# Windowed attention into a gated MLP: the third unit's transposes and outputs one step later, and both parts of the root's diagonal on VectorE

## The chip, the cores and the metric

The kernel runs on one core of a Trainium2 chip. The metric is device microseconds of one launch; the median of three runs is given. A profiled execution of its own supplies the trace that the text reads. Engines are named as in the profile: PE is TensorE's matmul stream, PEld its weight loads, DVE is VectorE, ACT ScalarE, POOL GpSimd, SP SyncE, which here issues the DMAs.

## The reference

```python
def reference(q, k, v, w_gate, w_val, w_out, rms_g):      # q, k, v: 8 x 8 heads x 576 x 64
    scores = q @ k.T / 8                                   # per batch and head
    # heads 0-3: keys 0..31 back; heads 4-7: keys 0, 4, 8, .. 124 back
    attn = softmax(where(mask, scores, -1e9))
    x = concat_heads(attn @ v)                             # 4608 tokens x 512
    xn = x / sqrt(mean(x * x, -1) + 1e-6) * rms_g
    g = xn @ w_gate                                        # 512 x 1536
    return (g * sigmoid(g) * (xn @ w_val)) @ w_out         # 1536 x 512
```

All is float32.

## The kernel before

The 4608 tokens are cut into 16 units of 288 (half a batch each). A unit has an attention part and an MLP part. The MLP of a unit takes 12 blocks j of 128 hidden columns, and each block takes three steps called ticks: a gate tick (12 matmuls into the PSUM tile g), a val tick (12 into v) and a projection tick (12 into the four accumulators acc, for the block before). The first unit (u = 0) uses float32 weights; from u = 1 on every product is made of three fp32r products of high and low parts (names ending in hi and lo).

The attention of unit u+1 runs inside the ticks of unit u's MLP. It consists of 14 bursts, one for each pair of heads and block of queries. A burst (c, i) passes through three stages on PE at three ticks: scores s (L509, or L512 from u = 3), transposes of the weights t (L487) and outputs o (L496, or L500 and L501). Lists of ticks set when: `q_at`, `t_at` and `o_at`. Units below NEX = 3 do their attention in plain float32, so "the third unit" (u = 2, NNAT = 2) is the last with float32 attention and the first whose attention runs beside fp32r MLP matmuls. Within a tick PE has the 12 MLP matmuls first, then the burst work.

What the other engines do for a tick is put off with `later(dt, rank, fn)`: at the start of a later tick `flush()` issues what is due, in order of rank. Ranks that matter here: a SwiGLU product (prod) has 0, the transposes' copy out of PSUM (untranspose, tile pt) 0.2, the addition of squares 0.4, the output copy (take, tile xraw) 0.5, silu 0.6, the maximum of the scores (scores_max, L379 and L384) 0.7. Each engine runs its own list strictly in order.

A transpose writes either into the free end of the g or v bank of that tick or, in a projection tick, into a PSUM tile of its own.

At the end of a unit's attention stands its root. `rms_sum` sums the squares on PE (rps, L560); `rms_root` adds epsilon on DVE (L567), takes the power -1/2 on POOL (rst, L568), and splits it on POOL into rst_hi (L573) and rst_lo (L574). `spread` makes of each part three 96 x 96 diagonals, the tiles rd_0 and rd_1, one on DVE (L582, one instruction) and one on ACT (L586, three instructions). Two matmuls with a matrix of ones (L602, bps) then broadcast the root over the partitions, and four DVE instructions (L616) scale x with it. The bps matmuls stand on PE behind the gate group of the eleventh block (g_10), two ticks after rps; the scores of a burst of the next attention (s_0_2) stand just ahead of g_10.

On POOL the root's two small instructions are followed by hlo (L723, low part of the hidden block) and by qs (L362, low part of a head's queries).

Of the kernel before, what the change touches and what calls it, by code (L numbers as in the profile page):

```python
# [9 lines left out]
F32 = mybir.dt.float32  # L10
# [3 lines left out]
AF = mybir.ActivationFunctionType  # L14
ALU = mybir.AluOpType
# [10 lines left out]
QB = 96  # L26
NC = DM // P
NJ = FF // P
NNAT = 2
NEX = 3  # L30
# [31 lines left out]
def geometry(u, c):  # L62


    half = u % 2
    if c < NC // 2:
        if half:
            return [(QB * i, QB * i, 0, P) for i in range(U // QB)], QB, U + W
        return [(QB * i, max(QB * i - W, 0), 0 if i else W, P if i else QB)
                for i in range(U // QB)], QB, U  # L70
    nq = U // DIL
    keys = nq + (W if half else 0)
    return [(nq * r, keys * r, 0 if half else W, keys) for r in range(DIL)], nq, keys * DIL
# [3 lines left out]
def attn_moe(ctx: ExitStack, tc: tile.TileContext, qk_in, v_in, w_gate, w_val, w_out, rms_g, outT):  # L77
# [4 lines left out]
    V, A, G, PE = nc.vector, nc.scalar, nc.gpsimd, nc.tensor  # L82
# [6 lines left out]
    ident = cst.tile([QB, QB], F32, name="ident")  # L89
# [29 lines left out]
    def later(dt, rank, fn):  # L119
        put_off.setdefault(now[0] + dt, []).append((rank, fn))  # L120
# [182 lines left out]
    def further(b, n):  # L303

        k = everything.index(b) + n
        return everything[k] if k < len(everything) else None
# [129 lines left out]
    def add(u, c, i, o):  # L436
        _, nq, _ = geometry(u, c)
        x = xraw[u, c]
        to = x[:, QB * i:QB * i + nq] if c < NC // 2 else x.rearrange("p (j r) -> p r j", r=DIL)[:, i, :]
        for a in range(2):  # L440
            rows = slice(a * D, (a + 1) * D)
            V.tensor_tensor(out=to[rows], in0=o[rows, a * nq:(a + 1) * nq], in1=to[rows], op=ALU.add)  # L442
# [18 lines left out]
    def untranspose(b, t_ps, wait):  # L461
        blocks, nq, _ = geometry(*b[:2])
        n = blocks[b[2]][3]
        t_in = t_ps[:n].rearrange("k (a q) -> k a q", a=2)[:, :, :nq]
        exact = b[0] < NEX
        st[b] = pt = sb.tile([P, 2, 2, QB], F32 if exact else F32R, tag="pt", name=f"pt_{b[0]}_{b[1]}_{b[2]}", bufs=2)
        A.copy(out=pt[:n, 0, :, :nq], in_=t_in)  # L467
        def low_part():
            V.tensor_tensor(out=pt[:n, 1, :, :nq], in0=t_in, in1=pt[:n, 0, :, :nq], op=ALU.subtract)

        if not exact:
            later(1, 0.4 if wait > 1 else -1.5, low_part) if wait else low_part()

    def products(q, t, o, t_ps, s_tag="s", o_tag="o", wait=0):


        if q:
            s_ps = ps.tile([P, 512], F32, tag=s_tag, name=f"s_{q[0]}_{q[1]}_{q[2]}")
        if o:
            o_ps = ps.tile([P, 512], F32, tag=o_tag, name=f"o_{o[0]}_{o[1]}_{o[2]}")  # L480
            pt = st.pop(o)
        if t:
            p, _ = st.pop(t)
        def transposed(a):
            blocks, nq, _ = geometry(*t[:2])
            n = blocks[t[2]][3]
            PE.transpose(t_ps[:n, a * QB:a * QB + nq], p[:nq, a, :n], ident[:nq, :nq])  # L487

        def output(a):
            blocks, nq, _ = geometry(*o[:2])  # L490
            n = blocks[o[2]][3]
            if a:
                return
            out = o_ps[:, :2 * nq].rearrange("d (a q) -> d a q", a=2)
            if o[0] < NEX:
                PE.matmul(out, vs.pop(o)[:n].rearrange("k a d -> k (a d)"), pt[:n, 0, :, :nq], start=True, stop=True)  # L496
                return
            vh, vl = (part[:n].rearrange("k a d -> k (a d)") for part in vparts[everything.index(o) % 2])
            both = o_ps[:, :4 * nq].rearrange("d (t a q) -> d t a q", t=2, a=2)
            PE.matmul(both, vh, pt[:n, :, :, :nq], start=True, stop=False)  # L500
            PE.matmul(out, vl, pt[:n, 0, :, :nq], start=False, stop=True)  # L501

        def scored(a):
            blocks, nq, _ = geometry(*q[:2])
            qc, kc, _, n = blocks[q[2]]
            sv = s_ps[:QB].rearrange("q (a t k) -> q a t k", a=2, t=2)
            if q[0] < NEX:
                qk = heads[q[0], 2 * q[1] + a]
                PE.matmul(sv[:nq, a, 0, :n], qk[:, qc:qc + nq], qk[:, U + kc:U + kc + n], start=True, stop=True)  # L509
                return  # L510
            qs, ks = heads[q[0], 2 * q[1] + a]
            PE.matmul(sv[:nq, a, :, :n], qs[:, qc:qc + nq], ks[:, :, kc:kc + n], start=True, stop=True)  # L512

        order = ((t, transposed), (o, output), (q, scored))
        if t and t[0] >= NEX:
            order = ((o, output), (t, transposed), (q, scored))
        parts = [(b, fn, a) for b, fn in order for a in range(2)]
        for b, fn, a in parts:
            if b:
                fn(a)  # L520
        if t:
            later(1, 0.2, lambda: untranspose(t, t_ps, wait))
        if o:
            later(1, 0.5, lambda: take(*o, o_ps))
            if o[0] >= NEX:
                later(2, -0.3, lambda: add(*o, o_ps))
            if o[0] < NEX:
                later(1, 9, lambda: load_v(further(o, 3)))
            far = further(o, 2)
            if far and far[0] >= NEX:  # L530
                split_v(far, 8 if o[0] < NEX else 1)
        if q:
            later(1, 0.7, lambda: scores_max(*q, s_ps))
            later(2, 0.42 if wait == 1 else 2, lambda: scores_exp(*q))
            later(3 if q[0] < NNAT else 4, -1, lambda: scores_norm(*q))
            u, c, i = q
            nxt = after(u, 2 * c, 2)
            nb = len(geometry(u, c)[0])
            if u < NEX:
                if u == NNAT - 1 and c == NC - 1 and i == nb - 1:  # L540
                    for h in range(4):
                        later(1, 9, lambda h=h: load(NNAT, h))
                if u >= NNAT and i == nb - 1 and c < NC - 1:
                    for a in range(2):
                        later(1, 9, lambda a=a: load(*after(u, 2 * c + a, 4)))
                if u == NEX - 1 and c == NC - 1 and i == nb - 1:
                    for a in range(2):
                        later(3 + a, 9, lambda a=a: split(NEX, a, (1, 2, 2, 3), G, G))
            elif nxt and i == 0:
                split(*nxt, (1, 2, 2, 3), G, G)  # L550
                split(nxt[0], nxt[1] + 1, (2, 3, 3, 4) if c < NC - 1 else (1, 2, 3, 4), G, G)

    xs = {}
    NB = U // QB
# [10 lines left out]
    def rms_root(u, r_ps):  # L565
        r = sb.tile([QB, NB], F32, tag="rst", name=f"rst_{u}", bufs=2)
        V.tensor_scalar(out=r, in0=r_ps[:, :, 0], scalar1=1e-6, scalar2=None, op0=ALU.add)  # L567
        G.tensor_tensor(out=r, in0=r, in1=mhalf, op=ALU.pow)  # L568
        if u == 0:
            rst[u] = [r]  # L570
            return
        r_hi, r_lo = (sb.tile([QB, NB], F32R, tag=f"rst_{p}", name=f"rst_{p}_{u}", bufs=1) for p in ("hi", "lo"))
        G.tensor_copy(out=r_hi, in_=r)  # L573
        G.tensor_tensor(out=r_lo, in0=r, in1=r_hi, op=ALU.subtract)  # L574
        rst[u] = []

        def spread():
            for p in (r_hi, r_lo):
                d = sb.tile([QB, NB, QB], F32R, tag="tmp", name=f"rd_{u}_{len(rst[u])}", bufs=2)
                rst[u].append(d)  # L580
                if p is r_hi:
                    V.tensor_tensor(out=d, in0=ident[:QB, None, :QB].to_broadcast([QB, NB, QB]),  # L582
                                    in1=p[:, :, None].bitcast(F32).to_broadcast([QB, NB, QB]), op=ALU.mult)
                    continue
                for i in range(NB):
                    A.activation(out=d[:, i, :], in_=ident, func=AF.Copy, scale=p[:, i:i + 1].bitcast(F32))  # L586
        later(1, 0.1, spread)

    def spread_first():
        r, = rst[0]  # L590
# [208 lines left out]
    for u in range(1, NU):  # L799
        q_at = [LAST - (LAST - EARLY) * (nb - 1 - k) // (nb - 1) for k in range(nb)]  # L800
        t_at, o_at = ([t + n for t in q_at] for n in BEHIND)
        if u <= NNAT:
            q_at = SCORES[u]
            t_at, o_at = [t + 5 for t in q_at], [t + (7 if u < NNAT else 8) for t in q_at]
        plan(u, ends - 2 + 3 * NJ * (u - 1), q_at, t_at, o_at)
    for n in range(ends):
        decode(STEPS[n])
# [18 lines left out]
    for u in range(NU):  # L826
        for j in range(NJ):
            for part in range(0 if u + j else 2, 3):
                t = 3 * (u * NJ + j) + part
# [95 lines left out]
```

## Time and profile before

| | us |
|---|---|
| median of 3 runs | 1116.42 (1116.35 to 1116.69) |
| profiled execution, its own time | 1116.57 |
| its span, first to last instruction | 1114.8 |
| PE busy | 1102.5 (99%) |
| PEld busy | 1076.9 (97%) |
| DVE busy | 670.9 (60%) |
| ACT busy | 708.8 (64%) |
| POOL busy | 674.7 (61%) |

The granted TensorE clock is 1.000 over the span. PE's busy share contains overlap of matmuls in flight, so what counts on PE is the distance from start to start and the places where a weight load (PEld) stood idle. In the rows of the timeline the first number is the start from the span's beginning, the second the duration in us, then engine, line, operation, output <- inputs, shape and how many like ones were merged; a bracket gives idle time before it and who ended it.

### The profile page before, as it was taken

To read this page: it belongs to the slowest core of one execution; us is meant where nothing else is said; L and a number is where in the kernel's file an instruction comes from. 1 tells how busy PE (TensorE), PEld (TensorE's weight loads), DVE (VectorE), ACT (ScalarE), POOL (GpSimd) and SP (SyncE) were. 2 spreads that over 40 slices of the span, in tenths; PEclk is the share of its full clock that TensorE was granted. 3 is DMA by queue.
4 is the path that set the end of the run, shared out by engine and by line. 5 is a ranking of instruction groups with operands and counts; after the bars stand their busy time and mean duration, and the time that the engine had idled before them with its cause. 6 is when DMAs were issued, how large, how long until landed. Compare 5 with 4: busy or idle time off the path is not lost.

```text
span 1114.8 us, 25463 instructions
## 1 busy us (share of the span) xinstructions
PE 1102.5 (99%) x8362; PEld 1076.9 (97%) x8362; DVE 670.9 (60%) x2734; ACT 708.8 (64%) x2579; POOL 674.7 (61%) x1154
## 2 busy tenths in 40 slices
PE   7999999999999999999999999999999999999998
PEld 5787999999999999999999999999999999999998
DVE  7889667656566564656656565665656656565312
ACT  6795676757576675767657576675757667575311
POOL 7423578756586665757657575675658657584211
PEclk9999999999999999999999999999999999999999
DMA  9665213212131121311212121131312212120000
GB/s 252 195 231 197 73 43 88 84 35 79 41 95 50 41 85 41 94 40 55 82 39 84 41 83 54 47 96 29 87 43 80 64 32 80 53 73 13 11 13 22
DMA packets 61542, 82.16 MB, mean 74 GB/s; under 512 B 7298, under 2 KB 41090, under 8 KB 61410
## 3 DMA queue, kind: packets, MB, share of 16 engines
q1 hardware_dynamic: 61410, 80.54, 24.4%
q8 instruction: 66, 1.08, 0.4%
q14 instruction: 66, 0.54, 0.2%
HBM read 71.08 MB, written 9.44 MB: 72 GB/s over the span
## 4 chain that ended last, share of the span: by engine, by line
PE 94%; POOL 2%; ACT 1%; DVE 1%; DMA 1%; issue 1%; SPq 0%; POOLq 0%; ACTq 0%; DVEq 0%
PE acc L656 17%; PE g L656 17%; PE v L656 17%; PE acc L653 9%; PE g L653 8%; PE v L653 8%; PE s L512 3%; PE o L500 3%; PE acc L650 2%; PE v L650 2%; PE g L650 2%; PE t L487 2%; PE o L501 1%; PE g L487 1%; PE o L496 1%; PE s L509 1%
## 5 line engine op out<-in xcount | busy, mean ns | idle before, releaser
L723 POOL TENSOR_TENSOR hlo<-th,hhi 128x288 fp32r<-128x288 f32 x179 | 145.7, 814 | 185.1 <-ACT hhi L722 169.9
L656 PE MATMUL acc<-hhi,lo 128*128 128x288 f32 x720 | 212.6, 295 | 0.0
L698 DVE SCALAR_TENSOR_TENSOR th<-th,g 128x288 f32<-128x288 f32 x180 | 81.8, 454 | 213.0 <-ACT pt L467 124.7
L395 ACT ACTIVATE t<-t,sum 96x128 f32<-96x128 f32 (+3 forms) x448 | 165.3, 372 | 33.5 <-DVE sum L384 32.0
L656 PE MATMUL g<-xhi,lo 128*128 128x288 f32 x612 | 180.3, 295 | 0.0
L656 PE MATMUL v<-xhi,lo 128*128 128x288 f32 x612 | 180.2, 294 | 0.0
L411 POOL TENSOR_SCALAR t<-t,sum 72x72 f32<-72x72 f32 (+3 forms) x414 | 152.2, 379 | 31.6 <-DVE sum L405 20.5
L693 ACT ACTIVATE th<-g 128x288 f32<-128x288 f32 x180 | 73.9, 411 | 151.3 <-PE g L487 59.0
L323 POOL TENSOR_TENSOR vlo<-vt,vhi 128x128 fp32r<-128x128 f32 x182 | 84.2, 463 | 116.7 <-ACT vhi L319 113.5
L656 PEld LDWEIGHTS acc<-hhi,lo 128*128 128x128 f32 x720 | 135.4, 188 | 0.0
L722 ACT CAST hhi<-th 128x288 fp32r<-128x288 f32 x180 | 77.8, 432 | 85.3 <-DVE th L711 84.7
L442 DVE TENSOR_TENSOR xraw<-o,xraw 64x72 f32<-64x72 f32 (+1 forms) x364 | 97.3, 267 | 42.0 <-ACT xraw L431 38.5
L656 PEld LDWEIGHTS v<-xhi,lo 128*128 128x128 f32 x612 | 115.1, 188 | 0.0
L656 PEld LDWEIGHTS g<-xhi,lo 128*128 128x128 f32 x612 | 115.1, 188 | 0.0
L711 DVE TENSOR_TENSOR th<-th,v 128x288 f32<-128x288 f32 x180 | 81.0, 450 | 54.7 <-PE v L656 53.0
L653 PE MATMUL acc<-hhi,hi_o 128*128 128x288 f32 x360 | 109.0, 303 | 0.0
L653 PE MATMUL g<-xhi,hi_g 128*128 128x288 f32 x357 | 106.8, 299 | 0.0
L656 PE MATMUL acc<-hlo,hi_o 128*128 128x288 f32 x360 | 106.4, 296 | 0.0
L431 ACT COPY xraw<-o 64x72 f32<-64x72 f32 (+1 forms) x364 | 95.5, 262 | 9.7 <-PE o L501 7.6
L353 POOL TENSOR_TENSOR ks<-qk,ks 128x288 fp32r<-128x288 f32 (+2 forms) x104 | 93.3, 901 | 3.1
L656 PE MATMUL g<-xlo,hi_g 128*128 128x288 f32 x322 | 95.1, 295 | 0.0
L362 POOL TENSOR_TENSOR qs<-qk,qs 64x288 fp32r<-64x288 f32 x104 | 84.2, 809 | 14.6 <-ACT qs L357 7.8
(188 smaller groups left out, 3522.2 us busy)
## 6 DMA issues: line engine op xcount, KB each, us to landing
qk<-in_qk_dram SPq DMA_DIRECT2D x60, 288.0 KB, 2.9
vt<-in_v_dram SPq DMA_DIRECT2D x196, 64.0 KB, 1.9
qk<-in_qk_dram SPq DMA_DIRECT2D x30, 352.0 KB, 3.0
out_dram<-ot SPq DMA_DIRECT2D x64, 144.0 KB, 1.9
qk<-in_qk_dram SPq DMA_DIRECT2D x30, 304.0 KB, 2.9
raw<-in_w_gate_dram SPq DMA_DIRECT2D x12, 512.0 KB, 5.7
raw<-in_w_val_dram SPq DMA_DIRECT2D x12, 512.0 KB, 5.5
raw<-in_w_out_dram SPq DMA_DIRECT2D x12, 512.0 KB, 4.2
```

The costliest lines, as they stand in the source:

```text
L323: G.tensor_tensor(out=vl, in0=vs.pop(b), in1=vh, op=ALU.subtract)
L353: ek.tensor_tensor(out=ks[:, 1, :nkt], in0=kr, in1=ks[:, 0, :nkt], op=ALU.subtract)
L362: eq.tensor_tensor(out=qs[D:], in0=qr[D:], in1=qs[D:], op=ALU.subtract)
L395: A.activation(out=t[:nq, a, :n], in_=t[:nq, a, :n], func=AF.Exp, scale=-1.0, bias=sm[:nq, a, 0:1], accum_out=sm[:nq, a, 1:2] if u or i % ...
L411: (V if u == 0 and (c, i) > (NC - 1, 0) else G).tensor_scalar(out=t[:nq, a, :n], in0=t[:nq, a, :n], scalar1=sm[:nq, a, 3:4], scalar2=1.0, ...
L431: A.copy(out=to[a * D:(a + 1) * D], in_=o[a * D:(a + 1) * D, (2 + a) * nq:(3 + a) * nq])
L442: V.tensor_tensor(out=to[rows], in0=o[rows, a * nq:(a + 1) * nq], in1=to[rows], op=ALU.add)
L653: PE.matmul(out, wh[:, cc, :], xh, start=start, stop=False)
L656: PE.matmul(out, w[:, cc, :], v, start=False, stop=stop and k == 1)
L698: V.scalar_tensor_tensor(out=t, in0=t, scalar=1.0, in1=g, op0=ALU.add, op1=ALU.mult)
L711: V.tensor_tensor(out=t, in0=t, in1=v_ps[:, :U], op=ALU.mult)
L723: (V if (u, j) == (NU - 1, NJ - 1) else G).tensor_tensor(out=lo, in0=t, in1=hi, op=ALU.subtract)
```

## The change

Three edits. In the third unit (u = 2) the transposes stand six ticks behind the scores instead of five, and the outputs nine instead of eight, and within a tick the output comes before the transposes (as it already does from u = 3 on). The scores of that unit lie in gate and val ticks; before, its transposes and outputs lay in projection and gate ticks, and now they lie in gate and val ticks too. In the root of every unit from u = 1 on, both diagonals are made by DVE, one instruction each, and `spread` has rank 0.75 instead of 0.1.

```diff
-        if t and t[0] >= NEX:
+        if t and t[0] >= NNAT:
             order = ((o, output), (t, transposed), (q, scored))
...
-                if p is r_hi:
-                    V.tensor_tensor(out=d, in0=ident[:QB, None, :QB].to_broadcast([QB, NB, QB]),
-                                    in1=p[:, :, None].bitcast(F32).to_broadcast([QB, NB, QB]), op=ALU.mult)
-                    continue
-                for i in range(NB):
-                    A.activation(out=d[:, i, :], in_=ident, func=AF.Copy, scale=p[:, i:i + 1].bitcast(F32))
-        later(1, 0.1, spread)
+                V.tensor_tensor(out=d, in0=ident[:QB, None, :QB].to_broadcast([QB, NB, QB]),
+                                in1=p[:, :, None].bitcast(F32).to_broadcast([QB, NB, QB]), op=ALU.mult)
+        later(1, 0.75, spread)
...
-            t_at, o_at = [t + 5 for t in q_at], [t + (7 if u < NNAT else 8) for t in q_at]
+            t_at, o_at = [t + 5 + u // NNAT for t in q_at], [t + (7 if u < NNAT else 9) for t in q_at]
```

PE in the third unit, from the float32 scores of burst (3, 1) to those of burst (3, 3), before; the 12 matmuls of a tick's group are left out as "...", t_4 is a transpose tile of its own in a projection tick, and g_5 the bank of a gate tick:

```order
L509 MATMUL s_3_1_1758<-qk_6_1462 72x72
...
L487 MATMUL t_4_1793<-ident,t_2_2_1631 72x72 x2
L496 MATMUL o_2_0_1794<-pt_2_0_1695,vt_2_0_1640 128x144
...
L487 MATMUL g_5_1810<-ident,t_2_3_1669 72x72 x2
L496 MATMUL o_2_1_1824<-pt_2_1_1732,vt_2_1_1704 128x144
L509 MATMUL s_3_2_1823<-qk_6_1462 72x72
L509 MATMUL s_3_2_1823<-qk_7_1464 72x72
...
L509 MATMUL s_3_3_1862<-qk_6_1462 72x72
```

The same place now:

```order
L496 MATMUL o_2_0_1805<-pt_2_0_1716,vt_2_0_1667 128x144
L487 MATMUL g_5_1791<-ident,t_2_2_1615 72x72 x2
L509 MATMUL s_3_2_1804<-qk_6_1459 72x72
L509 MATMUL s_3_2_1804<-qk_7_1461 72x72
...
L496 MATMUL o_2_1_1846<-pt_2_1_1754,vt_2_1_1727 128x144
L487 MATMUL v_5_1832<-ident,t_2_3_1660 72x72 x2
L509 MATMUL s_3_3_1845<-qk_6_1459 72x72
```

The work of the projection tick moved into the gate tick and that of the gate tick into the val tick, where the transposes now share v's bank; the projection ticks have none left.

DVE at the root of unit u = 3, from the product of block 9 to the silu of block 10, before:

```order
L711 TENSOR_TENSOR th_9_3286<-th_9_3286,v_9_3300 128x288
L567 TENSOR_SCALAR rst_3322<-rps_3313 96x3
L582 TENSOR_TENSOR rd_0_3353<-ident,rst_hi_3325 96x288
L379 TENSOR_TENSOR t_0_2_3359<-s_0_2_3350,mask 96x256
L384 ISA t_0_2_3359,sum_89<-s_0_2_3350,t_0_2_3359 96x128
L384 ISA sum_89 96x1
L404 TENSOR_REDUCE sum_88<-sum_88 96x2
L405 RECIPROCAL sum_88<-sum_88 96x2
L698 SCALAR_TENSOR_TENSOR th_10_3383<-th_10_3383,g_10_3363 128x288
```

and now (line numbers behind the edit are four smaller; the pair of L384 rows comes twice in both and is shown once):

```order
L567 TENSOR_SCALAR rst_3311<-rps_3302 96x3
L379 TENSOR_TENSOR t_0_2_3342<-s_0_2_3339,mask 96x256
L384 ISA t_0_2_3342,sum_89<-s_0_2_3339,t_0_2_3342 96x128
L384 ISA sum_89 96x1
L581 TENSOR_TENSOR rd_0_3346<-ident,rst_hi_3314 96x288
L581 TENSOR_TENSOR rd_1_3348<-ident,rst_lo_3315 96x288
L404 TENSOR_REDUCE sum_88<-sum_88 96x2
L694 SCALAR_TENSOR_TENSOR th_10_3370<-th_10_3370,g_10_3350 128x288
```

The diagonals moved from ahead of the scores' maximum to behind it, and the second one came over from ACT. The order is the same in every root from u = 2 to u = 14. At u = 1 and in the last unit no scores stand there, and the diagonals keep their place.

## Prediction

> **What bounds the kernel now.** I read the page first: PE holds nearly the whole chain of work that ended last.
>
> ```profile
> PE 94%; POOL 2%; ACT 1%; DVE 1%; DMA 1%; issue 1%; SPq 0%; POOLq 0%; ACTq 0%; DVEq 0%
> ```
>
> So a change counts only where it alters the distance between PE's instructions, or makes PE wait. Next I read PEld's waits, since a wait that holds PE shows there first; of those that this change can touch, this is the largest sum.
>
> ```profile
> PEld bps L602 <- ACT rd L586: 0.8, 2, 0.6
> ```
>
> From the second unit's MLP on PE is packed; the time is decided at two kinds of place: the ticks of the third unit's attention, and the fourteen later roots.
>
> **The third unit's ticks.** PE's timeline there (start, duration):
>
> ```profile
> 148.13 0.29 PE L487 MATMUL t<-ident,t 72*72 72x72 f32 x2
> 148.26 0.46 PE L496 MATMUL o<-pt,vt 72*128 72x144 f32 x2
> ...
> 152.47 0.42 PE L509 MATMUL s<-qk 128*72 128x72 f32 x4
> 152.69 0.38 PE L653 MATMUL acc<-hhi,hi_o 128*128 128x288 f32 x1
> 152.90 0.29 PE L656 MATMUL acc<-hlo,hi_o 128*128 128x288 f32 x1
> ...
> 154.36 0.29 PE L487 MATMUL t<-ident,t 72*72 72x72 f32 x2
> ...
> 158.40 0.30 PE L653 MATMUL acc<-hhi,hi_o 128*128 128x288 f32 x1
> ...
> 160.00 0.29 PE L487 MATMUL t<-ident,t 72*72 72x72 f32 x2
> ...
> 166.02 0.41 PE L496 MATMUL o<-pt,vt 72*128 72x144 f32 x2
> 166.17 0.39 PE L653 MATMUL g<-xhi,hi_g 128*128 128x288 f32 x1
> 166.40 0.29 PE L656 MATMUL g<-xlo,hi_g 128*128 128x288 f32 x1
> ```
>
> One block of three ticks takes 6.23 (148.13 to 154.36). A clean group of 12 takes 1.60 (158.40 to 160.00), or 0.13 a matmul. Scores cost 0.22 to the next start, and 0.08 more because the first fp32r matmul after them takes 0.21 instead of 0.13: 0.30. An output behind a group costs 0.15 plus 0.10 of the same kind: 0.25. A pair of transposes takes 0.13. The new block is 3 x 1.60 + 2 x (0.25 + 0.13 + 0.30) = 6.16, so 0.07 less; about six blocks: -0.4. The bounds are 0 (the order of pieces is all the same) and -0.6 (seven returns to fp32r fewer, at the 0.08 to 0.10 above).
>
> One stall stands in this stretch: an output waits for ACT to have copied the output before.
>
> ```profile
> 162.49 0.30 PEld L496 LDWEIGHTS o<-pt,vt 72*128 72x128 f32 x2 [0.36 <-ACT xraw L428]
> ```
>
> With outputs and scores now in the same ticks the copy gets the scores' 0.3 more; I take -0.36, bounds 0 and -0.36. The change adds a wait here: in a val tick the transposes share v's bank, so ACT's copy of them stands behind DVE's product, and the gate group two ticks later needs that bank. One projection group (1.60) lies between as cover. If it isn't enough, hhi and the next tanh queue behind the copy on ACT, and PE waits. I take 0, and up to +0.36 once (the largest wait on ACT of this stretch) for the range. The later outputs also move the last squares of this unit by one tick; they had more than a tick in hand, and POOL's part of the root stood in its own queue anyway (next rows). The loads of the third unit's last values and of the next heads change places on SP, each needed several ticks later: 0.
>
> **The third unit's root.**
>
> ```profile
> 176.93 0.86 POOL L568 TENSOR_TENSOR rst<-rst,mhalf 96x3 f32<-96x3 f32 x1
> 178.08 0.46 DVE L582 TENSOR_TENSOR rd<-ident,rst_hi 96x288 fp32r<-96x288 f32 x1 [2.21 <-POOL rst_hi L573]
> 178.13 0.46 POOL L574 TENSOR_TENSOR rst_lo<-rst,rst_hi 96x3 fp32r<-96x3 f32 x1
> 178.56 0.79 POOL L723 TENSOR_TENSOR hlo<-th,hhi 128x288 fp32r<-128x288 f32 x1
> 178.62 0.91 ACT L586 ACTIVATE rd<-ident,rst_lo 96x96 fp32r<-96x96 f32 x3 [2.35 <-POOL rst_lo L574]
> 179.58 0.19 PEld L602 LDWEIGHTS bps<-rd,ones 96*128 96x128 f32 x1 [0.63 <-ACT rd L586]
> ```
>
> Here PE waits 0.63 for ACT's diagonal (end 179.53, weight load 0.05 later; I use 0.05 for each hand-over). DVE stood idle 2.21 ahead of its own, so the scores fit in there and rd_0 stays at 178.08. rd_1 can start at 178.62, but hlo has begun: what that costs is worked out below, and gives 179.72 for the second bps, 0.14 later than now, if POOL's queue doesn't move. Then the 0.76 won before is waited away here. If POOL moves along with PE, 0.76 less 0.14 stays. No row shows how much of POOL's queue hangs on PE's pace; I take the middle, -0.2 for the whole third unit, with +0.5 and -0.6 as ends.
>
> **The other roots.** Two forms alternate. Unit u = 3 for the first, u = 4 for the second, and the last of each form (six of each, u = 3 to 14):
>
> ```profile
> 244.32 0.40 PE L512 MATMUL s<-ks,qs 128*96 128x256 f32 x2
> 244.68 0.46 DVE L582 TENSOR_TENSOR rd<-ident,rst_hi 96x288 fp32r<-96x288 f32 x1 [1.46 <-POOL rst_hi L573]
> 244.73 0.46 POOL L574 TENSOR_TENSOR rst_lo<-rst,rst_hi 96x3 fp32r<-96x3 f32 x1
> 245.06 0.41 DVE L379 TENSOR_TENSOR t<-s,mask 96x256 f32<-96x256 f32 x1
> 245.16 0.81 POOL L723 TENSOR_TENSOR hlo<-th,hhi 128x288 fp32r<-128x288 f32 x1
> ...
> 245.93 0.15 DVE L404 TENSOR_REDUCE sum<-sum 96x2 f32<-96x4 f32 x1
> 246.02 0.35 PEld L602 LDWEIGHTS bps<-rd,ones 96*128 96x128 f32 x2
> 246.04 0.80 POOL L362 TENSOR_TENSOR qs<-qk,qs 64x288 fp32r<-64x288 f32 x1
> ```
>
> ```profile
> 310.65 0.40 PE L512 MATMUL s<-ks,qs 128*96 128x256 f32 x2
> 311.24 0.46 POOL L574 TENSOR_TENSOR rst_lo<-rst,rst_hi 96x3 fp32r<-96x3 f32 x1
> 312.69 0.19 PEld L602 LDWEIGHTS bps<-rd,ones 96*128 96x128 f32 x1 [0.16 <-ACT rd L586]
> ```
>
> ```profile
> 911.38 0.35 PEld L602 LDWEIGHTS bps<-rd,ones 96*128 96x128 f32 x2
> 977.65 0.46 PEld L602 LDWEIGHTS bps<-rd,ones 96*128 96x128 f32 x2
> ```
>
> Now DVE can begin its diagonals only behind the maximum of scores that PE finishes at 244.72. First form: L379 at 244.77; from L379 to what follows the maximum is 0.87 (245.06 to 245.93), so rd_0 at 245.64, ended 246.10; rd_1 begins 0.38 after rd_0 (244.68 to 245.06), ends 246.48, second bps at 246.53. Before, that load began at 246.18 (246.02 + 0.35 less the 0.19 of one). PE waits 0.35 longer. Second form, scores done at 311.05: 312.86 against 312.69, 0.17. So with nothing in the way twelve roots cost 6 x 0.52 = 3.1. Covered before by nothing but those tenths, the diagonal is late from the start.
>
> **What is in the way: POOL.** Two-input instructions of DVE and POOL stretch each other:
>
> ```profile
> L574 POOL TENSOR_TENSOR rst_lo<-rst,rst_hi x15: 190/460/463, 102.7 to 1042.5; 96x3 fp32r<-96x3 f32 x15
> ```
>
> ```profile
> 171.13 1.58 DVE L252 TENSOR_TENSOR lo<-f,hi_g 128x512 fp32r<-128x512 f32 x1
> 172.12 1.26 POOL L723 TENSOR_TENSOR hlo<-th,hhi 128x288 fp32r<-128x288 f32 x1
> 172.63 1.07 DVE L454 TENSOR_TENSOR sq<-sq,sq 128x288 f32<-128x288 f32 x1
> ...
> 148.66 1.79 POOL L454 TENSOR_TENSOR sq<-sq,sq 128x288 f32<-128x288 f32 x1
> 148.77 0.68 DVE L252 TENSOR_TENSOR lo<-f,hi_g 128x512 fp32r<-128x512 f32 x1
> 149.38 0.42 DVE L251 CAST hi_v<-f 128x512 fp32r<-128x512 f32 x1
> ```
>
> The tiny rst_lo takes 0.19 at best and 0.46 under a diagonal. At 172 the engines take turns: POOL's hlo ends 0.67 after DVE's lo (173.38, 172.71), and DVE's waiting squares 0.32 after hlo (173.70). At 148 they don't: DVE's cast goes straight behind its lo, and POOL waits through both.
>
> By turns, first form: without a diagonal beside it rst_lo takes 0.19, hlo runs 244.89 to 245.70, qs starts at 245.77 and is held by rd_0 until 246.10, ends 0.67 later at 246.77, rd_1 at 247.09, second bps at 247.14: 0.96 late. Second form: hlo ends 312.21, rd_0 312.53, qs 313.20, rd_1 313.52, bps 313.57: 0.88 late. Sum 6 x 1.84 = 11.0. (At the third unit, rd_1 behind hlo's end 179.35: 179.67 and 0.05.) If DVE keeps its turn, rd_1 ends 246.48 and, after the held rd_0, 312.91: 0.35 and 0.27, sum 3.7. If hlo keeps its present time, the same working gives 1.15 and 1.14: 13.7. I take turns, since 172 has two two-input DVE instructions in a row as rd_0 and rd_1 are, and 148 has a cast second.
>
> The Trainium skill (SBUF — State Buffer, Who interferes with whom) says that a DVE instruction with two SBUF inputs contends with a GpSimd one that reads SBUF, and that whoever issues first holds the shared port for its whole instruction. By that rule qs, issued ahead of rd_1, goes first and the sum is the 11.0; the rows at 172 agree, those at 148, where POOL issued first and went last, do not.
>
> ACT is freed of 0.91 a root, and nobody waits for ACT there any more. Behind rd_1 on DVE wait the reduce and silu of block 10; its product is needed on PE a val group and a projection group later (over 3 us): 0. qs ends later by some 0.7; its scores come several ticks on: 0. The second unit's and the last root have no scores in front and a full group in hand: 0.
>
> **Sum.** Against the profiled execution's 1116.57: -0.2 + 11.0 = 1127.4; the median is 0.15 lower, so 1127.2.
>
> **Rivals.** (1) DVE keeps its turn: -0.2 + 3.7, so 1119.9; for it the rows at 148, against it those at 172. (2) Faster: the diagonals run the moment POOL gives rst_lo, ahead of the scores' maximum. rd_1 then needs 0.46 instead of ACT's 0.91, the third unit's 0.63 and six waits of up to 0.16 go, with the 0.76: 2.3 in all, 1114.1. It decides at 1.41 after the end of the scores, when the diagonal must be done to be no later than now; L379 to L404 alone takes 0.87 and rd_0 and rd_1 0.84. The order of DVE's rows speaks against it. (3) The change does not do what it says: what is won in the third unit and lost at the roots cancel, 1116 to 1118. It needs the smallest loss (3.1) and the whole gain.
>
> **How the numbers follow.** Forecast 0.68, rival 1 0.20, rival 2 0.04, rival 3 0.08. A measurement here can tell about 0.2%, 2.2 us. Slower takes the forecast and rival 1, 0.88; same 0.08; faster 0.04. The forecast's own range is 1125 to 1130.5 (hlo not earlier, and the third unit's bad end); the range reaches down to rival 1's low end, 3.1 - 0.6: 1118.9.
>
> **What would show it.** In the profile after: PEld waits at bps for DVE rd in every root from u = 3 to 14, near 0.9 each (turns) or 0.3; rd_0 starting 0.9 after the scores, not at rst_hi; rd_1 or qs drawn out to over 1 us; rst_lo near 0.19; blocks of 6.16 and no 0.36 stall in the third unit. I am wrong if DVE's rows show the diagonals ahead of L379, or if bps does not wait.

## The result and the profile after

The changed kernel takes 1137.02 us (median of 6 runs, 1136.49 to 1137.62), the kernel before 1116.73 beside it (6 runs). The ratio is 1.0174, with an interval of 1.0164 to 1.0185: 20.3 us slower, where 10.8 had been forecast.

The chain of waits of the changed kernel now has VectorE in it, and PE's share fell from 94% to 92%:

```profile
PE 92%; DVE 4%; ACT 1%; POOL 1%; issue 1%; DMA 1%; SPq 0%; DVEq 0%; POOLq 0%
```

PEld's waits after (engine, who waits, for whom; sum, times, longest, all in us). The first row was foreseen, at 13 roots; its waits are up to 0.7 where near 0.9 each had been given. The other three belong to the third unit. Of these, the wait for xraw stood in the prediction as one stall of 0.36 that would go, and the wait for pt as a possible one of up to 0.36. The waits of the scores for VectorE, the largest of the three, had no place in it:

```profile
PEld bps L598 <- DVE rd L581: 9.4, 13, 0.7
PEld s L509 <- DVE sum L384: 7.3, 10, 1.1
...
PEld o L496 <- ACT xraw L428: 2.3, 5, 1.3
...
PEld g L649 <- ACT pt L467: 0.6, 1, 0.6
```

**The roots.** The timeline after at the root of u = 3 (start, duration), to be held against the rows of 244 to 246 of before:

```profile
254.11 0.40 PE L512 MATMUL s<-ks,qs 128*96 128x256 f32 x2
...
254.53 0.19 POOL L574 TENSOR_TENSOR rst_lo<-rst,rst_hi 96x3 fp32r<-96x3 f32 x1
254.55 0.42 DVE L379 TENSOR_TENSOR t<-s,mask 96x256 f32<-96x256 f32 x1 [1.53 <-PE s L512]
...
254.69 0.81 POOL L719 TENSOR_TENSOR hlo<-th,hhi 128x288 fp32r<-128x288 f32 x1
...
255.43 0.45 DVE L581 TENSOR_TENSOR rd<-ident,rst_hi 96x288 fp32r<-96x288 f32 x1
...
255.57 0.96 POOL L362 TENSOR_TENSOR qs<-qk,qs 64x288 fp32r<-64x288 f32 x1
...
255.80 1.05 DVE L581 TENSOR_TENSOR rd<-ident,rst_lo 96x288 fp32r<-96x288 f32 x1
...
256.90 0.19 PEld L598 LDWEIGHTS bps<-rd,ones 96*128 96x128 f32 x1 [0.72 <-DVE rd L581]
```

Read it downwards: rst_lo is back at 0.19, rd_0 stands 0.9 behind the maximum's start, qs slips in while rd_0 runs and ends at 256.53, and rd_1 ends 0.32 behind qs. PE waits 0.72 for it. The load of the second bps begins 2.39 behind the end of the scores (254.51), where before it began 1.46 behind them: 0.93 later, where 0.96 had been worked out. In the second form, at u = 4, rd_0 takes 0.70 beside hlo, rd_1 takes 1.04 beside qs, and that load is 0.99 later; 0.88 had been worked out.

**The third unit.** The timeline at one of its gate ticks. PE has done the output and the transposes and then stands still until VectorE's maximum, which itself had waited 3.04 for those transposes:

```profile
147.65 0.49 PE L496 MATMUL o<-pt,vt 128*128 128x192 f32 x2
...
147.97 0.29 PE L487 MATMUL g<-ident,t 72*72 72x72 f32 x2
...
148.30 0.23 DVE L384 CUSTOM_DVE_ANT_0 t<-s,mask 72x72 f32<-72x72 f32 x1 [3.04 <-PE g L487]
...
148.46 0.22 DVE L384 CUSTOM_DVE_ANT_0 t<-s,mask 72x72 f32<-72x72 f32 x1
...
148.74 0.33 PEld L509 LDWEIGHTS s<-qk 128*72 128x72 f32 x4 [0.65 <-DVE sum L384]
...
155.65 0.41 PE L496 MATMUL o<-pt,vt 72*128 72x144 f32 x2
```

A block here takes 8.00 (147.65 to 155.65) where 6.16 was forecast. Why should the maximum of one burst wait for the transposes of another? Because it writes a buffer from which they read. The lines, which the prediction did not look at (the second is shortened where "..." stands):

```python
other = u < NNAT and everything.index((u, c, i)) % 4 == 3                    # L376
t = sb.tile([QB, 2, P], F32, tag="qs" if other else "t", ..., bufs=3)        # L377
```

In the first two units every fourth burst keeps its weights t in buffers of another tag, so a buffer of t comes back after four bursts. In the third unit it comes back after three. There are two bursts in three ticks. Take the bursts scored at ticks 4, 6, 7 and 9: the last one's maximum writes the buffer of the first. Five ticks behind its scores, that one's transposes stood in tick 9 itself, and were done. Six ticks behind they stand in tick 10, the very tick in which PE scores the next burst. These scores need the one PSUM tile s, which the waiting maximum still has to read. So PE itself runs through the loop in each such tick: transposes, maximum, scores. (From u = 3 on a burst is scored every second tick, and six ticks are three bursts: there the same distance fits.)

The kernel before shows a beginning of it, in projection ticks, where the transposes of five ticks behind lie and no scores follow, so that PE lost nothing there. Six rows between 122 and 155 have it, with VectorE idle for 0.86 to 2.02. This one is from the kernel before's timeline; the bracket shows VectorE held by the transposes:

```profile
148.46 0.23 DVE L384 CUSTOM_DVE_ANT_0 t<-s,mask 72x72 f32<-72x72 f32 x1 [1.10 <-PE t L487]
```

**Where the time went.** To divide the 20 us, three stretches of each profiled execution: from the second unit's root (start of L567 for u = 1) to the third's; from there to PE's first weight load behind the bps of u = 2 (179.69 before, 189.50 after); and from there to the same place of u = 14, twelve roots later.

| | third unit's attention | its root | twelve roots |
|---|---|---|---|
| before | 74.78 | 3.97 | 798.34 |
| after | 84.59 | 4.36 | 808.95 |
| difference | +9.81 | +0.39 | +10.61 |

The three make 20.8; the spans differ by 20.5 (1135.3 and 1114.8), since what lies ahead of the first stretch was 0.4 shorter. A stretch is not the same in every execution. With the root as before, five of them (this one and four of the experiments below) give 798.23 to 799.45 for the twelve roots; with the changed root, four give 808.75 to 808.96. So the twelve roots cost 9.3 to 10.7, and a difference of about 1 in this column says little. The third unit's attention with its old ticks takes 74.78 to 75.01 in three of them.

### The profile page after: what moved, and what is told of

Its sections match the earlier page's. It is cut to its first block, busy times and chain, and to the rows that moved or that the text cites. A ratio compares the mean times of both kernels' runs of the same rounds, so it can differ in the third digit from the quotient of the medians.

```text
span 1135.3 us, 25458 instructions
## 1 busy us (share of the span) xinstructions
PE 1110.6 (98%) x8362; PEld 1078.4 (95%) x8362; DVE 681.3 (60%) x2749; ACT 695.3 (61%) x2534; POOL 673.8 (59%) x1154
## 4 chain that ended last, share of the span: by engine, by line
PE 92%; DVE 4%; ACT 1%; POOL 1%; issue 1%; DMA 1%; SPq 0%; DVEq 0%; POOLq 0%
PE acc L652 17%; PE v L652 16%; PE g L652 16%; PE acc L649 9%; PE v L649 8%; PE g L649 8%; PE s L512 3%; PE o L500 2%; PE acc L646 2%; PE v L646 2%; PE g L646 2%; DVE rd L581 2%; PE t L487 2%; PE o L501 1%; PE g L487 1%; PE o L496 1%
```

## Experiments

Each is compared with the kernel before on the same chip; behind a time stand the ratio and its 95% interval.

**The two halves apart.** First the root's edit alone, then the third unit's alone (each the diff's own lines on the kernel before).

> The kernel before with only the root's edit (both diagonals on VectorE, rank 0.75). The 20.3 us lost are two things that have nothing to do with each other: twelve roots by turns with GpSimd, and something in the third unit. Then this one alone gives 1116.7 + about 10 = 1126.7 (0.88 at six first-form roots and 0.78 at six second-form ones, read off the trace after), and the third unit has its old blocks of 6.23 us. Rival: the third unit's waits come from the root's edit (VectorE's list is longer there): then nearly all of the 20 shows here, 1135.

> The kernel before with only the third unit's edit (order of pieces, ticks 6 and 9). By the theory of two separate losses it gives 1116.7 + about 9 to 10 = 1126, with some ten waits of PE's weight loads at the scores (L509) for VectorE's maximum (L384) of 0.65 us each. By the rival the waits need the root's edit and the time is 1116 to 1117.

Measured: the root alone 1128.13 (ratio 1.0098, 1.0073 to 1.0122), the third unit alone 1126.68 (1.0083, 1.0061 to 1.0105). Over the same runs of before (1117.41) that is +10.7 and +9.3, together 20.0. With the root alone the third unit's attention takes 74.87, as before, and its root 4.81 instead of 3.97; with the third unit alone the attention takes 84.51 and the root 3.57. The waits of each half stay in its own kernel. PEld's waits, root alone and then third unit alone:

```profile
PEld bps L598 <- DVE rd L581: 9.4, 13, 0.7
```

```profile
PEld s L509 <- DVE sum L384: 7.3, 10, 1.2
...
PEld o L496 <- ACT xraw L428: 2.3, 5, 1.3
```

So there are two separate losses, and the longer list of VectorE at the root has nothing to do with the third unit.

**A fourth buffer for t, and the old order.** The first is the changed kernel with

```diff
-        other = u < NNAT and everything.index((u, c, i)) % 4 == 3
+        other = u <= NNAT and everything.index((u, c, i)) % 4 == 3
```

and the second the changed kernel with `if t and t[0] >= NEX:` put back in products.

> The changed kernel, with the weights tile t of every fourth burst of the third unit in another pool's buffers, as the two units before have it: a burst's t then reuses the buffer of the burst four before, not three. Theory: the maximum of burst k writes t into the buffer of burst k-3, whose transposes now stand in the very tick of the scores k+1, and these wait on PE for the maximum of burst k since there is one PSUM tile s; so PE waits 0.65 in every such tick. With four buffers that chain is cut: the waits of L509 vanish, and the time falls by the third unit's 9.4 us or a little more, to 1127. Rival: VectorE or ScalarE is simply late in these ticks (silu, product and the copies queue up): the waits stay and the time is 1137.

> The changed kernel, but in the third unit the transposes again stand ahead of the output within a tick (ticks 6 and 9 kept). By the theory of the buffer of t the scores still wait, but the output (0.25 to 0.33 us) now lies between transposes and scores and covers a part of the 0.65: about ten waits of 0.35 instead of 0.65, so 1137 less 3 = 1134. By the rival (the order outputs first is what costs) the waits are gone: 1127.

Measured: 1125.89 with the fourth buffer (1.0074, 1.0054 to 1.0095), 1134.57 with the old order (1.0162, 1.0132 to 1.0192). Both go the way the theory has it; the first is 1.1 below the 1127 expected. With the fourth buffer no score of this unit waits for the maximum. In its timeline the scores follow the transposes at once, and the maximum comes later:

```profile
148.17 0.41 PE L496 MATMUL o<-pt,vt 72*128 72x144 f32 x2
148.42 0.29 PE L487 MATMUL g<-ident,t 72*72 72x72 f32 x2
148.54 0.42 PE L509 MATMUL s<-qk 128*72 128x72 f32 x4
...
149.83 0.22 DVE L384 CUSTOM_DVE_ANT_0 t<-s,mask 72x72 f32<-72x72 f32 x1
```

The waits for ScalarE went with the loop (2.3 to 0.3, and the 0.6 altogether). That they came from exp, which waits for the late maximum while the copies stand behind it on ScalarE, fits this but was not tried by itself. With the old order the output covers a part of the loop. PEld's waits there:

```profile
PEld s L509 <- DVE sum L384: 5.1, 10, 1.1
...
PEld g L649 <- ACT pt L467: 2.1, 4, 1.1
```

**The order alone, at the old ticks.** The kernel before with only `t[0] >= NNAT` in products.

> The kernel before with the output ahead of the transposes in the third unit, at the old ticks (5 and 8). By the theory of the buffer of t the ticks are the cause: no wait of the scores for the maximum appears, and the time is 1116 to 1117. Rival: the order lets the scores come straight behind the transposes, and that alone makes them wait: 1120 or more.

Measured: 1116.80 (1.0003, 0.9992 to 1.0013). The order is worth nothing by itself, and with the old order the later ticks still lose; so the later ticks, with three buffers, are the cause.

**The third unit repaired, root as before.** The kernel before with the third unit's edit and the fourth buffer, run twice.

> The kernel before with the third unit's edit and the fourth buffer of t, the root left as it was (rd_0 on VectorE, rd_1 on ScalarE, rank 0.1). If the two losses are separate and the fourth buffer cures the first, what remains is the third unit's edit without its flaw: the profile of the fourth-buffer run has the third unit's root at 173.98 us, where before it stood at 175.72, so 1.7 less, 1115.0 against 1116.7; and if the wait of 0.63 at that root stays as before, no more than that. If the third unit's gain is waited away at its root (rst behind GpSimd's queue): 1116.5.

> Again the kernel with the third unit's edit, the fourth buffer and the old root, for a narrower interval: 1115.9, ratio 0.999.

Measured: 1115.94 (0.9991, 0.9980 to 1.0002), and the second time 1115.16 (0.9982, 0.9973 to 0.9991). Against before in the same comparison (1116.98 and 1116.85) that is 1.0 and 1.7 less: some 0.1 to 0.2%, and not better known. The stretches say where it is: third unit's attention 74.05 and 73.99 (before 74.78), its root 3.55 and 3.51 (3.97).

**What makes rd_1 slow.** Here qs of the root's tick goes to VectorE, ahead of the maximum; the rest is the changed kernel with the fourth buffer.

```diff
-                split(nxt[0], nxt[1] + 1, (2, 3, 3, 4) if c < NC - 1 else (1, 2, 3, 4), G, G)
+                split(nxt[0], nxt[1] + 1, (2, 3, 3, 4) if c < NC - 1 else (1, 2, 3, 4), G, G if c else V)
```

> The changed kernel with the fourth buffer, and with qs of the root's tick (low part of a head's queries) made by VectorE ahead of the scores' maximum instead of by GpSimd behind hlo, so that GpSimd has no two-input instruction to put between rd_0 and rd_1. Theory (turns on the shared path): rd_1 takes 0.46 instead of 1.05 in all twelve roots, the waits at the second bps fall by 0.6 each, 12 x 0.6 = 7.2: 1125.9 - 7.2 = 1118.7. Rival: rd_1 is slow for a reason of its own (it reads the part that GpSimd has just written, or VectorE's queue): it stays 1.05 and the time 1126.

Measured: 1121.87 (1.0046, 1.0032 to 1.0059), between the two expectations. The timeline at the root of u = 3 shows why:

```profile
244.24 0.19 POOL L574 TENSOR_TENSOR rst_lo<-rst,rst_hi 96x3 fp32r<-96x3 f32 x1
244.39 0.80 POOL L719 TENSOR_TENSOR hlo<-th,hhi 128x288 fp32r<-128x288 f32 x1
244.85 0.65 DVE L581 TENSOR_TENSOR rd<-ident,rst_hi 96x288 fp32r<-96x288 f32 x1
245.43 0.44 DVE L581 TENSOR_TENSOR rd<-ident,rst_lo 96x288 fp32r<-96x288 f32 x1
```

rd_1 is at 0.44, as the theory has it. But the maximum now starts earlier against hlo, so rd_0 is the one that waits its turn: it ends 0.31 behind hlo. My expectation counted only qs and forgot hlo. The twelve roots take 804.91 here, 4.0 less than in the changed kernel.

**Without any turn, at both ranks.** Both hlo of that block and qs go to VectorE, in the idle time ahead of rd_0. The edit beside the one above:

```diff
-            (V if (u, j) == (NU - 1, NJ - 1) else G).tensor_tensor(out=lo, in0=t, in1=hi, op=ALU.subtract)
+            (V if (u, j) == (NU - 1, NJ - 1) or j == 9 else G).tensor_tensor(out=lo, in0=t, in1=hi, op=ALU.subtract)
```

once with rank 0.75 as in the change, once with 0.1 as before.

> The same with rank 0.75: the changed root with nothing of GpSimd's in its way. This is the term that the prediction worked out as 6 x 0.35 + 6 x 0.17 = 3.1 for a diagonal behind the maximum of the scores without any turn: 1115.9 + 3.1 = 1119. If moving rd_1 to VectorE costs what it does without GpSimd: 1126.

> The changed kernel with the fourth buffer, rank 0.1, and both hlo of block 10 and qs of the root's tick made by VectorE in the idle time ahead of rd_0, so that GpSimd has no two-input instruction behind rst_lo. By the theory of turns rd_1 takes 0.46 straight behind rst_lo, ends 0.97 behind the end of rst_hi, 0.45 earlier than ScalarE's did, and no bps waits at all: with the waits of 0.1 to 0.14 at the second-form roots (six) and 0.29 at the third unit's gone, 1115.9 - 1.1 = 1114.8. If rd_1 is slow in itself: as with rank 0.1 and GpSimd's work in place, 1116.7. If VectorE is too late with the two added instructions (0.9 us), rd_0 starts later than rst_hi and the time is over 1118.

Measured: at rank 0.75 1117.85 (1.0008, 0.9999 to 1.0017), at rank 0.1 1113.66 (0.9967, 0.9955 to 0.9980). The second is the fastest version of this case: 1.5 below the repaired third unit with the old root beside it (1115.16). How much of this is the turns, and how much that GpSimd has two instructions less to do, was not tried apart. The first is 1.2 below its expected 1119. The group of rd_1 by shape (count, then ns least/median/most), after and then at rank 0.75 without turns:

```profile
L581 DVE TENSOR_TENSOR rd<-ident,rst_lo x15: 440/1045/1052, 102.9 to 1063.6; 96x288 fp32r<-96x288 f32 x15
```

```profile
L581 DVE TENSOR_TENSOR rd<-ident,rst_lo x15: 441/447/455, 102.7 to 1044.1; 96x288 fp32r<-96x288 f32 x15
```

With nothing in the way the late diagonals cost 801.49 - 798.34 = 3.15 over the twelve roots; the prediction's working gave 3.1. Against the other executions with the old root it is 2.0 to 3.3, so that the agreement to a tenth is luck. What the turns add is steadier, 7.3 to 7.5 (808.75 to 808.96 less 801.49). At rank 0.1 the same timeline place reads

```profile
241.26 0.46 DVE L719 TENSOR_TENSOR hlo<-th,hhi 128x288 fp32r<-128x288 f32 x1 [0.43 <-ACT hhi L718]
241.75 0.46 DVE L362 TENSOR_TENSOR qs<-qk,qs 64x288 fp32r<-64x288 f32 x1
242.30 0.45 DVE L581 TENSOR_TENSOR rd<-ident,rst_hi 96x288 fp32r<-96x288 f32 x1
...
242.84 0.45 DVE L581 TENSOR_TENSOR rd<-ident,rst_lo 96x288 fp32r<-96x288 f32 x1
```

Each of the two low parts takes 0.46 on VectorE against 0.8 on GpSimd, no bps waits for a diagonal any more, and the twelve roots take 797.35, 0.9 to 2.1 less than with the old root.

**The rank and the engine, one at a time** (both with the fourth buffer): rd_1 back on ScalarE at rank 0.75, and both diagonals on VectorE at rank 0.1 with GpSimd's work in its old place.

> The changed kernel with the fourth buffer, but rd_1 back on ScalarE, at the changed rank 0.75: only the rank differs from the kernel before at the root. If the loss is rd_1's turn behind qs on VectorE, the rank alone costs little: rd_0 ends 1.3 behind the scores, the first bps is 0.1 to 0.2 late, and the time is 1115 + 12 x 0.15 = 1117. Rival: the rank is the loss, whoever makes the diagonal: 1122 or more. ScalarE's list at rank 0.75 has nothing long ahead of rd_1.

> The changed kernel with the fourth buffer, both diagonals on VectorE but at the old rank 0.1, ahead of the scores' maximum. By turns hlo, issued by GpSimd straight behind rst_lo, goes ahead of rd_1, which ends 0.32 behind it: about 0.2 later than ScalarE's was in each of twelve roots, 1115 + 2.4 = 1117.5. If VectorE keeps its turn instead, rd_1 ends 0.46 behind rst_lo, earlier than ScalarE's 0.91: 1114. If the rank does not matter: 1126.

Measured: 1117.29 (1.0005, 0.9996 to 1.0014) and 1116.71 (1.0000, 0.9991 to 1.0009). Neither engine nor rank loses the 10 alone. The twelve roots take 800.25 and 800.07, which is 0.6 to 2.0 more than with the old root. At rank 0.1 hlo takes the turn ahead of rd_1, but there are no scores in front, so the diagonal is late by little:

```profile
242.77 0.46 POOL L574 TENSOR_TENSOR rst_lo<-rst,rst_hi 96x3 fp32r<-96x3 f32 x1
243.19 0.81 POOL L719 TENSOR_TENSOR hlo<-th,hhi 128x288 fp32r<-128x288 f32 x1
243.26 1.05 DVE L581 TENSOR_TENSOR rd<-ident,rst_lo 96x288 fp32r<-96x288 f32 x1
```

## Why the prediction was right and wrong

- **The twelve roots, 11.0: right, 10.61 in this pair of profiles and 9.3 to 10.7 over all.** By the steps: rd_0 behind the maximum, qs taking the turn, rd_1 0.32 behind qs, rst_lo at 0.19. The part without turns (3.1 against 2.0 to 3.3) was measured by taking the turns away, and the turns are the rest. Rival 1, VectorE keeping its turn, fell: rd_1 takes 1.04 to 1.05 in all roots of u = 2 to 14. The rule of the Trainium skill that the prediction cited (SBUF — State Buffer, Who interferes with whom), the first to issue keeps the port for its whole instruction, fits all three places shown: qs waits for rd_0 (0.96 instead of 0.80), rd_1 for qs (1.05), and with qs gone rd_0 for hlo (0.65). By the starts that the profile shows, the cast at 166.59 below does not fit it.
- **The third unit, -0.2: wrong, and this is the step that failed.** It measured +9.81 and +0.39 at its root. The prediction followed what the later ticks do to the PSUM banks and to ScalarE's copies, and went through no SBUF buffer. It took the maximum of the scores as a thing that the transposes do not touch, and the row of 148.46 before, where VectorE waits 1.10 for them, was not read. In its place the runs showed a loop over the buffer of t: PE's scores wait ten times for VectorE's maximum (7.3 in sum) and the maximum waits for PE's transposes; with a fourth buffer these waits are gone, and the third unit's attention takes 74.02 instead of 84.59. The wait that it did price (the bank of v, up to 0.36) came once, with 0.6, and it goes when the buffer is there.
- **The sum of that step holds once the buffer is there, and part of that is luck.** Blocks of 6.16 in place of 6.23 and the stall of 0.36 were to give -0.76; with the fourth buffer and the old root the third unit's attention measures -0.73 and -0.79. But a stall of 0.26 of that kind is left at 162, and a block takes 6.12 to 6.13 (148.17 to 154.29 with the fourth buffer, 148.59 to 154.72 with the old root beside it). So the blocks gave more than was worked out and the stall less.
- **The third unit's root: mis-sized.** The prediction let the scores' maximum fit in ahead of rd_0, and priced the diagonals at 0.14. In the runs the maximum waits for PE's scores until 186.85, and rd_0 starts 0.72 behind the end of rst_hi (187.73 against 187.01), where before it started 0.04 behind it. The diagonals cost 0.84 there with the old ticks (4.81 against 3.97), and 0.83 to 0.87 with the new ticks and the fourth buffer (4.38 against 3.55 and 3.51). What the prediction left open, whether GpSimd's queue moves along with PE, came out well: rst starts 0.76 to 0.81 behind L567 with the third unit's edit, and 1.21 behind it before. The +0.39 of the table is the difference of the two.
- **Rival 2, 1114.1, by diagonals ahead of the maximum.** The change is not that kernel, as the order of VectorE's rows had said. But a kernel that does what this rival says, with the fourth buffer and with hlo and qs out of the way on VectorE, came out at 1113.66.
- **The range.** Its ends were made of bounds on the terms that stood in the sum. The missing term, 9.8 in the third unit's attention, was in none of them, so no end could reach it.

## What to carry to other kernels

When a stage is moved later, count for every tile between producer and consumer how many buffers it has, and divide. Here, with three buffers and two bursts in three ticks, the transposes could stand five ticks behind the scores and not six. A bracket on the writer's row that names the old reader as its releaser was the sign of a buffer at its limit, even where the wait cost nothing yet. And two instructions of VectorE in a row, each with two SBUF inputs, let a GpSimd instruction in between here, in every root from u = 2 on. What helped was to put the neighbour's work ahead, into VectorE's idle time (801.49 for the twelve roots in place of 808.75), or to leave one of the two on ScalarE (800.25).

## What the runs showed of the hardware

The prediction had held a cast on VectorE apart from two-input instructions, since at 148 one went ahead of GpSimd. In the trace after the same cast of 128x512 took 1.73 instead of 0.42 beside a GpSimd subtraction that began 0.16 later; it ended at 168.32, that one at 168.03. The timeline after:

```profile
166.59 1.73 DVE L251 CAST hi_o<-f 128x512 fp32r<-128x512 f32 x1
...
166.75 1.28 POOL L252 TENSOR_TENSOR lo<-f,hi_o 128x512 fp32r<-128x512 f32 x1
```

So a cast from SBUF to SBUF can lose its turn too. The kernel before had shown it, and the prediction did not use it: at 124.54 a cast of the same shape takes 1.08 and ends 0.28 behind a GpSimd subtraction that began at 124.06. Why the cast at 148 did not wait was not tried.
